# A scheduled attention and mixer kernel: a shorter chain for 64-bit weights, and merged softmax operations

## The chip, the core and the metric

The kernel runs on one core of one Trainium2 chip. The core has a matrix engine (TensorE; its weight loads are a row of their own, PEld, in the profile), a vector engine (VectorE, DVE in the profile), a scalar engine (ScalarE, ACT), GpSimd (POOL) and SyncE (SP), which only issues transfers here. The metric is the device time of one launch in microseconds. Shown are the median of three runs before the change, 1540.35 us, and their ends, 1537.54 and 1543.84 us.

## The reference

Three stages follow one another. All weight matrices and U, V come in 64-bit floats, everything else in 32-bit.

```python
def sm_attn(qq, kk, vv):                       # scale = 1/8
    s = scale * np.matmul(qq, kk.transpose(0, 1, 3, 2))
    a = np.exp(s - np.max(s, axis=-1, keepdims=True))
    a = a / (np.sum(a, axis=-1, keepdims=True) + 1e-09)
    return np.matmul(a, vv)
p_packed = sm_attn(p, k, v)                    # first softmax: 32 packed queries, 576 keys
out = sm_attn(q, p_packed, p_packed)           # second softmax: 576 queries, 32 keys
# out: batch 8, heads 8, 576, 64  ->  x: 8, 576, 512
xk = mu_k * x + (1.0 - mu_k) * x_prev          # x_prev: x shifted by one position
xr = mu_r * x + (1.0 - mu_r) * x_prev
k = np.maximum(xk @ w_k, 0.0)                  # 512 -> 1024
x = 1.0 / (1.0 + np.exp(-(xr @ w_r))) * (k * k @ w_v)
u = x + (x.transpose(0, 2, 1) @ U @ V).transpose(0, 2, 1)     # rank 32 over the positions
return u + np.maximum(u @ w_ch1, 0.0) @ w_ch2  # 512 -> 2048 -> 512
```

## The kernel before

The batches are taken in four pairs. One attention unit is a pair of batches and a pair of heads, so there are 16 units, four to a batch pair. A unit (`attention_steps`) loads k, q and v, transposes them on TensorE, forms the scores of the packed queries in two PSUM banks, takes the first softmax (statistics in the small tile `st`, exponentials in `a1`), multiplies by v to get the packed values `pp`, and then takes the second softmax: 20 groups of 32 keys, 16 of them in one PSUM bank (`psa`) and 4 in another (`psb`), with statistics in `s2` (`s` in the trace) and exponentials in `a2` (`a` in the trace). The output `xo` goes to a scratch array `x_d`. The first four units, those of batch pair 0, run beside one another, staggered; the other twelve run beside the stages that follow.

The second stage works on 12 chunks of 384 rows. It reads `x_d` back (`x`), mixes it (`m`, `xk`, `xr`), and runs matmuls into `psr`, `psk` and `psv`. A chunk needs all four units of its pair, since its contraction is over all heads. The third stage (`psu`, `psh`, `pst`, `psc`) starts at about 739 us of the trace.

A float matrix is used as two parts, `hi` and `lo`, in a rounded 32-bit format, and three products of parts stand for one product. A 64-bit weight reaches that form in the class `Cast`: a transfer brings a tile of 128 rows and 512 64-bit words into a staging buffer `st` (two of them, in rotation, so a third load waits until the first buffer has had its last reader), then a chain of ScalarE and VectorE operations builds the 32-bit value `m` from the high words (`hb`, `top`) and the low words of each number. Twenty tiles (w_r 4, w_k 8, w_v 8) end in a pair of parts (`parts` given); `split` makes these from `m`. Another 32 tiles (w_ch1, w_ch2) and the three pieces of U and V end in `m` itself (`put` given), which for w_ch1 and w_ch2 is stored to scratch and split much later. The name `st` in the trace thus is two things: the 128x512 staging buffer and the narrow statistics tile of the first softmax; and `a` is three (the softmax exponentials and the scratch of the conversion); shapes tell them apart.

No engine order is written out by hand. The program records operations with what they read and write, and `Plan.emit` runs a list scheduler over them with its own table of durations per engine, classes of priority (`cls`), and the banks of PSUM; in this way each engine gets one fixed order of instructions. On SyncE the order is fixed too, so a load that has to wait for its buffer holds up everything that stands behind it. A change of one operation's number or length can thus change the order on all engines.

ScalarE holds one table of functions at a time; `Exp` and `Sigmoid` are in different ones, and an `ACT_TABLE_LOAD` stands between them.

Of the kernel before, what the change touches and what calls it, by code (L numbers as in the profile page):

```python
# [9 lines left out]
F32 = mybir.dt.float32  # L10
F32R = mybir.dt.float32r
I32 = mybir.dt.int32
U32 = mybir.dt.uint32
AF = mybir.ActivationFunctionType
ALU = mybir.AluOpType
# [85 lines left out]
class Plan:  # L101
# [151 lines left out]

    def ts(self, out, a, s1, s2, op0, op1=None, engs=("dve",), cls=None):
        k = {} if op1 is None else {"op1": op1}
        return self.elem(
            engs, lambda e, o, x: e.tensor_scalar(out=o, in0=x, scalar1=s1, scalar2=s2, op0=op0, **k),
            out, [a], self.TC, cls)
# [212 lines left out]
def packed_attention_moe_mixer_kernel(  # L471
# [19 lines left out]
    NP = p.shape[2]  # L491
    P = 128
# [12 lines left out]
    SCALE = 1.0 / float(D) ** 0.5  # L505
# [3 lines left out]
    plan = Plan(nc)  # L509
    add, sub, mul = ALU.add, ALU.subtract, ALU.mult  # L510

    def open_pool(es, name, bufs, side):
        return es.enter_context(tc.tile_pool(name=name, bufs=bufs, side=side, reuse_waits="tile"))
# [19 lines left out]
    def ctile(name, shape, dt=F32):  # L533
        return plan.fixed(const.tile(shape, dt, name=name))

    ident = ctile("ident", [P, P])
    hmask = ctile("hmask", [P, 2, D])
# [8 lines left out]
    def ps_att():  # L546
        return plan.bank(att_banks[0], "psat", att_banks[0] is ps_a)
# [17 lines left out]
    class Bufs:  # L565
        def __init__(self, es, name, side, nbig, first=False):
            self.big_p = Pool(obj=open_pool(es, name + "big", nbig, side), bufs=nbig)
            one = open_pool(es, name + "one", 1, side)
            self.one = Pool(obj=one, bufs=1)
            self.a1 = plan.fixed(one.tile([P, 640], F32, name="a1"))  # L570
            self.pbd = plan.fixed(one.tile([P, 2, D], F32, name="pbd"))
            self.first = first
            self.pools = [self.big_p, self.one]
            for f in (self.a1, self.pbd):
                f.alloc = plan.add((), lambda: None)
                self.one.tiles.append(f)
            self.kin, self.qin, self.vin, self.after = {}, {}, {}, ()
            plan.zero(self.a1[:, 512:640])
            self.kept = None

        def keep(self, plain):
# [53 lines left out]
    def attention_steps(A, u, u_next):  # L635
# [35 lines left out]
        if u_next is not None:  # L671
            A.load_k(u_next, A.after)

        st = plan.tile(A.one, [P, 16], F32, "st", parts=(0, 1))
        yield
        sps = [ps_att() for _ in range(2)]
        for b2 in range(2):
            for h in range(2):
                o = slice(b2 * 64 + h * 32, b2 * 64 + (h + 1) * 32)
# [5 lines left out]
        for b2 in range(2):  # L685
            for h in range(2):
                o = slice(b2 * 64 + h * 32, b2 * 64 + (h + 1) * 32)
                plan.mm(sps[0][o, 256:320], pT[0:64, b2, h * 32:(h + 1) * 32],
                        kt[0:64, h, b2 * 64:(b2 + 1) * 64], start=True, stop=True, skip_group_check=True)
        plan.reduce(st[:, 0:1], sps[0][:, 0:320], ALU.max)  # L690
        plan.reduce(st[:, 1:2], sps[1][:, 0:256], ALU.max)
        plan.tt(st[:, 2:3], st[:, 0:1], st[:, 1:2], ALU.max)
        plan.ts(st[:, 3:4], st[:, 2:3], -SCALE, None, mul)
        a1 = A.a1
        bias = st.at(0)[:, 3:4]
        for r in range(2):
# [3 lines left out]
        for b2 in range(2):  # L700
            r = slice(b2 * 64, (b2 + 1) * 64)
            plan.act(a1[r, 512 + b2 * 64:576 + b2 * 64], sps[0][r, 256:320], AF.Exp,
                     st.at(1)[r, 6:7], bias[r], SCALE)
        plan.reduce(st[:, 7:8], st[:, 4:7], add)
        plan.ts(st[:, 8:9], st[:, 7:8], 1e-9, None, add)
        plan.recip(st[:, 9:10], st[:, 8:9])

        for c in range(3):
            yield
# [25 lines left out]
        for t in range(5):  # L735
            for g in range(4):
                o = t * P + g * 32
# [3 lines left out]
                        start=(t == 0), stop=(t == 4), skip_group_check=True)  # L741
        pp = plan.tile(A.one, [P, P], F32, "pp")
        plan.stt(pp.rearrange("p (h d) -> p h d", h=2), ps[:, 0:D].unsqueeze(1).to_broadcast([P, 2, D]),
                 st[:, 9:10], hmask, mul, mul)
        plan.copy(ppz[:, 0, :], pp)
        if not plain:
            plan.tt(ppz[:, 1, :], pp, ppz[:, 0, :], sub)
# [18 lines left out]
        if A.first:  # L766
            a2 = A.big(F32, "a2", (0, 1))[:, 0:20 * NP].rearrange("p (g k) -> p g k", k=NP)
        else:
            a2 = plan.tile(A.one, [P, 20, NP], F32, "a2", parts=(0, 1))
        s2 = plan.tile(A.one, [P, 4, 20], F32, "s2", parts=(0, 1))  # L770
        for g, src, g0, g1 in ((0, psa, 0, 16), (1, psb[:, 0:P], 16, 20)):
            sv = src.rearrange("p (g k) -> p g k", k=NP)
            av, s = a2.on(g)[:, g0:g1, :], s2.at(g)
            bc = [P, g1 - g0, NP]
            plan.reduce(s[:, 0, g0:g1], sv, ALU.max)
            plan.tt(av, sv, s[:, 0, g0:g1].unsqueeze(2).to_broadcast(bc), sub)
            plan.act(av, av, AF.Exp, scale=SCALE)
            plan.reduce(s[:, 1, g0:g1], av, add)
            plan.ts(s[:, 2, g0:g1], s[:, 1, g0:g1], 1e-9, None, add)
            plan.recip(s[:, 3, g0:g1], s[:, 2, g0:g1])  # L780
            plan.tt(av, av, s[:, 3, g0:g1].unsqueeze(2).to_broadcast(bc), mul)

        a2f = a2.on(0).rearrange("p g k -> p (g k)")
        a2g = a2.on(1).rearrange("p g k -> p (g k)")
        th = A.big(F32 if plain else F32R, "th")
        tl = None if plain else A.big(F32R, "tl")
        yield
# [26 lines left out]
    def attention(A, u, u_next):  # L814
        for _ in attention_steps(A, u, u_next):
            pass


    class Cast:
# [7 lines left out]
        def run(self, srcs, n, put=None, parts=None, after=()):  # L827
            N = self.N
            raw = srcs[0][1].dtype != F32
            st = plan.tile(self.st, [P, N * 2], I32, "st", parts=tuple(range(len(srcs))))  # L830
            for i, (rows, src) in enumerate(srcs):
                s = st.at(i)
                to = s[rows, 0:2 * n] if raw else s[rows, 0:n].bitcast(F32)
                if raw:
                    src = src.bitcast(I32)
                if src.shape[0] > P:
                    to = to.rearrange("p (a c) -> p a c", a=src.shape[0] // P)
                    src = src.rearrange("(a p) c -> p a c", p=P)
                plan.dma(to, src, after=after)
            if not raw:  # L840
                if parts is None:
                    put(st.bitcast(F32))
                else:
                    split(*parts, st.bitcast(F32)[:, 0:n])
                return st.alloc
            r = slice(srcs[0][0].start, srcs[-1][0].stop)
            sv = st.rearrange("p (n t) -> p n t", t=2)[r, 0:n]
            whole = [plan.tile(self.tp, [P, N], F32, tag) for tag in "am"]
            a, m = [t[r, 0:n] for t in whole]
            top = h = sv[:, :, 1].bitcast(F32)  # L850
            plan.act(a, top, AF.Abs)
            plan.stt(h, a, 1.125 * 2.0 ** -15, top, ALU.is_ge, mul)
            plan.act(m, sv[:, :, 0].bitcast(U32), AF.Copy, scale=2.0 ** -52)
            hb, ab = sv[:, :, 1], a.bitcast(I32)
            plan.ts(ab, hb, 3, 0x3FFFFFF8, ALU.logical_shift_left, ALU.bitwise_and)
            plan.stt(ab, hb, -0x40000000, ab, ALU.bitwise_and, ALU.bitwise_or)
            plan.ts(hb, ab, -0x800000, None, ALU.bitwise_and)
            plan.tt(m, m, h, mul)
            plan.tt(m, m, a, add)
            if parts is None:  # L860
                put(whole[1])
            else:
                split(*parts, m)
            return st.alloc

    def split(hi, lo, src, engs=("dve",)):
        plan.copy(hi, src, ("act", "dve"))
        plan.tt(lo, src, hi, sub, engs)
# [42 lines left out]
    plan.cls = 0  # L911
    A0.after = go
    steps = [attention_steps(AX_[u], u, NJ if u == 0 else None) for u in range(NJ)]
    step = 0
    while any(s is not None for s in steps):
# [181 lines left out]
    def tmp_tile():  # L1097
        i = count["tmp"] % 6
        count["tmp"] += 1
        if i < 2:  # L1100
            return plan.tile(m_p, [P, CW], F32, "m", name="tmp")[:, 0:256]
        return plan.tile(tr_p, [P, 256], F32, "tmp")
# [114 lines left out]
    def product(q, f, i, name, fresh):  # L1217

        if fresh:
            bank_abc[name] = plan.bank(ps_c1, "psc1")  # L1220
        ps = bank_abc[name][:, 0:256]
        w, x = load_ws(f, i), ops[q][i]
        n = 0
        for k in range(2):
            for wi, a in PASS:
                plan.mm(ps, half(w, wi)[:, k * P:(k + 1) * P],
                        half(x, a)[:, k * 256:(k + 1) * 256],
                        start=(fresh and n == 0), stop=(n == 5), skip_group_check=True)
                n += 1
        return ps  # L1230
# [114 lines left out]
    for q in range(NQ):  # L1345
# [11 lines left out]
        for f in range(NF):  # L1357
# [4 lines left out]
            a = product(q, f, 0, "a", True)  # L1362
# [3 lines left out]
            s = tmp_tile()  # L1366
# [70 lines left out]
```

## Time and profile before

| What | Value |
|---|---|
| median of three runs | 1540.35 us (1537.54 to 1543.84) |
| span of the profiled execution, first to last instruction | 1538.1 us |
| TensorE busy | 1491.3 us, 97% of the span |
| VectorE busy | 962.4 us, 63% |
| ScalarE busy | 707.1 us, 46% |
| loads of 64-bit tiles on SyncE up to 175 us | 20, the first five of them before 40 us |

The page gives no time of the profiled execution other than its span, which lies 2.25 us under the median of the runs. The shares are means over stages with different limits. The page's line of 40 slices (38.5 us each) shows the stages apart: TensorE has gaps in the first four or five slices and hardly any after. A row of instruction groups gives busy time and the mean of one instruction, and then the idle time of the engine before it. Instructions of one engine overlap at their ends, so that the distance from start to start is a little shorter than the time of one.

### The profile page before, as it was taken

What the parts mean: (1) busy time and instruction counts of PE and PEld (TensorE: products, weight loads), DVE (VectorE), ACT (ScalarE), POOL (GpSimd) and SP (SyncE); (2) the same over time, 40 slices, a digit from 0 to 9 for tenths busy, and PEclk for the clock granted to TensorE, in tenths of its full rate; (3) what the DMA queues carried; (4) which work ended last, traced back from release to release, by engine and by line L of the source; (5) the groups of instructions that cost most, each with busy time, mean ns of one, the idle gap of its engine ahead of it and who ended that gap; (6) DMA issues with size and microseconds to landing.
All of it is one profiled execution on the core that took longest, in us unless ns stands there. A gap on an engine that the chain in (4) does not pass through costs nothing.

```text
span 1538.1 us, 25958 instructions
## 1 busy us (share of the span) xinstructions
PE 1491.3 (97%) x9460; PEld 1303.1 (85%) x9460; DVE 962.4 (63%) x2221; ACT 707.1 (46%) x1635; POOL 270.3 (18%) x522
## 2 busy tenths in 40 slices
PE   6779899999999999999999999999999999999998
PEld 4657688888888888888899999999999899999997
DVE  6888877888778886875745454444535354444533
ACT  5777657656756765665522232323222232322221
POOL 0000000000000000001233333333333333333331
PEclk9779999999999999999999999999999999999999
DMA  9865455555555444656877767686866767676763
GB/s 232 206 156 147 122 141 159 155 165 153 160 149 154 139 152 144 223 206 209 263 178 217 190 172 221 166 239 160 230 165 188 203 166 225 161 219 157 205 170 101
DMA packets 202174, 275.67 MB, mean 179 GB/s; under 512 B 68928, under 2 KB 95872, under 8 KB 202048
## 3 DMA queue, kind: packets, MB, share of 16 engines
q0 software_dynamic: 72576, 132.15, 33.0%
q1 hardware_dynamic: 129472, 141.87, 31.1%
q8 instruction: 76, 1.25, 0.3%
q14 instruction: 50, 0.41, 0.1%
HBM read 221.45 MB, written 52.50 MB: 178 GB/s over the span
## 4 chain that ended last, share of the span: by engine, by line
PE 91%; DMA 3%; DVE 2%; SPq 2%; ACT 2%; issue 1%; DVEq 0%
PE psc L197 49%; PE psk L197 13%; PE psv L197 13%; PE psr L197 6%; PE psat L197 4%; PE psat L209 2%; SPq L312 2%; PE psu L197 1%; PE psh L197 1%; PE pst L209 1%; DMA vin<-in_v_dram 1%; DMA s<-w_d 1%; DMA st<-in_moe_w_k_dram 0%; ACT a L230 0%; DMA kin<-in_k_dram 0%
## 5 line engine op out<-in xcount | busy, mean ns | idle before, releaser
L197 PE MATMUL psc<-w,hid 128*128 128x512 f32 x1728 | 446.2, 393 | 1.3 <-ACT xu L281 1.3
L197 PEld LDWEIGHTS psc<-ob,wb 128*128 128x128 f32 x3024 | 406.9, 190 | 26.7
L197 PE MATMUL psc<-ob,wb 128*128 128x256 f32 x3024 | 420.8, 283 | 0.0
L312 POOL DMA_DIRECT2D wb<-ws_d x504 | 267.2, 531 | 593.6 <-PE psc L197 498.6
L197 PEld LDWEIGHTS psc<-w,hid 128*128 128x128 f32 x1728 | 306.2, 189 | 52.0 <-ACT xu L281 1.6
L197 PE MATMUL psk<-xk,wk 128*128 128x384 f32 x1152 | 232.3, 344 | 3.4 <-ACT sq L230 2.4
L197 PE MATMUL psv<-wv,kk 128*128 128x512 f32 x864 | 231.7, 402 | 3.7 <-DVE wv L251 2.2
L197 PEld LDWEIGHTS psk<-xk,wk 128*128 128x128 f32 x1152 | 202.4, 189 | 13.9 <-ACT sq L230 3.3
L251 DVE TENSOR_TENSOR tmp<-tmp,psc 128x256 f32<-128x256 f32 x288 | 120.5, 419 | 143.4 <-PE psc L197 142.2
L230 ACT ACTIVATE hid<-tmp 128x256 fp32r<-128x256 f32 x216 | 85.2, 417 | 262.9 <-DVE tmp L251 262.7
L197 PEld LDWEIGHTS psv<-wv,kk 128*128 128x128 f32 x864 | 157.4, 189 | 37.9 <-DVE wv L251 4.2
L266 DVE SCALAR_TENSOR_TENSOR hid<-psc,hid 128x256 fp32r<-128x256 f32 x72 | 30.5, 424 | 188.3 <-ACT hid L230 188.3
L197 PE MATMUL psr<-wr,xr 128*128 128x512 f32 x432 | 114.7, 408 | 6.9 <-ACT r L281 2.7
L281 ACT ACTIVATE tmp<-psc 128x256 f32<-128x256 f32 x144 | 54.6, 379 | 126.5 <-PE psc L197 126.5
L197 PEld LDWEIGHTS psr<-wr,xr 128*128 128x128 f32 x432 | 80.7, 193 | 26.5 <-ACT r L281 3.8
L266 DVE SCALAR_TENSOR_TENSOR hid<-tmp,hid 128x256 fp32r<-128x256 f32 x216 | 86.3, 422 | 23.6 <-ACT hid L230 19.1
L304 POOL MEMSET x<- 128x8 f32 x4 | 0.5, 134 | 563.6 <-DVE m L263 385.9
L251 DVE TENSOR_TENSOR kk<-sq,kk 128x384 fp32r<-128x384 f32 x96 | 52.6, 552 | 41.3 <-ACT kk L281 41.1
L230 ACT ACTIVATE sq<-psk 128x384 f32<-128x384 f32 x96 | 46.4, 487 | 67.8 <-PE psk L197 66.9
L230 ACT ACTIVATE hid<-psc 128x256 fp32r<-128x256 f32 x72 | 27.5, 382 | 102.6 <-PE psc L197 102.6
L263 DVE SCALAR_TENSOR_TENSOR m<-x,mu_t,m 128x384 f32<-128x384 f32 x96 | 57.8, 611 | 6.6 <-ACT m L230 6.4
L230 ACT ACTIVATE m<-x,om_t 128x384 f32<-128x384 f32 x96 | 57.3, 610 | 7.5 <-DVE xk L251 3.8
(152 smaller groups left out, 1670.4 us busy)
## 6 DMA issues: line engine op xcount, KB each, us to landing
wb<-ws_d POOLq DMA_DIRECT2D x504, 256.0 KB, 3.1
st<-in_moe_w_ch_dram SPq DMA_DIRECT2D x32, 512.0 KB, 4.3
ws_d<-wb SPq DMA_DIRECT2D x56, 256.0 KB, 3.2
qin<-in_q_dram SPq DMA_DIRECT2D x32, 288.0 KB, 5.7
x_d<-xo SPq DMA_DIRECT2D x16, 576.0 KB, 3.1
x_d<-x SPq DMA_DIRECT2D x36, 256.0 KB, 3.4
u<-x_d SPq DMA_DIRECT2D x36, 256.0 KB, 5.8
out_dram<-u SPq DMA_DIRECT2D x36, 256.0 KB, 3.6
```

What stands on the lines that cost most here:

```text
L197: self.nc.tensor.matmul(o, l, r, start=start, stop=stop, **k)
L209: self.nc.tensor.transpose(out.get(), in_.get(), ident.get())
L230: self.nc.scalar.activation(o, in_.get(), func, **k)
L251: return self.elem(engs, lambda e, o, x, y: e.tensor_tensor(out=o, in0=x, in1=y, op=op), out, [a, b], self.TT, cls)
L263: ("dve",), lambda e, o, x, y, z: e.scalar_tensor_tensor(out=o, in0=x, scalar=z, in1=y, op0=op0, op1=op1), out, [a, b, s], {"dve": (1.042, ...
L266: ("dve",), lambda e, o, x, y: e.scalar_tensor_tensor(out=o, in0=x, scalar=s, in1=y, op0=op0, op1=op1), out, [a, b], self.TT, cls)
L281: self.nc.scalar.activation(o, i, AF.Copy)
L304: (self.nc.gpsimd if eng == "pool" else self.nc.vector).memset(o, 0.0)
L312: (self.nc.sync if eng == "sp" else self.nc.gpsimd).dma_start(out=o, in_=i)
```

## The change

The conversion: the comparison that set small numbers to zero becomes a maximum against the same constant, and the multiplication by the high word's float value moves into the last step. For a weight with parts, `hi` is no longer rounded from the finished value but built from the high word with its low bits masked off, and `lo` from the 9 bits left over plus the low word. ScalarE no longer converts the low words. In that form both the masked word and the low words stay in the staging buffer until the chain's last operation, which reads `top`.

The first softmax: `st` is a fixed tile; two small operations become one with a second scalar operand, and the constant 1e-9 stands in a fourth column of the sums. The second softmax: maximum and subtraction stay in two groups (16 and 4), everything after them is one operation over all 20.

```diff
@@ Plan.ts @@
+        if isinstance(s1, Ref):
+            return self.elem(
+                engs, lambda e, o, x, y: e.tensor_scalar(out=o, in0=x, scalar1=y, scalar2=s2, op0=op0, **k),
+                out, [a, s1], self.TC, cls)
...
@@ Bufs.__init__ @@
+            self.st = plan.fixed(one.tile([P, 16], F32, name="st"), (0, 1))
...
+            plan.ts(self.st.at(1)[:, 7:8], self.a1[:, 512:513], 1e-9, None, add)
...
@@ attention_steps, Cast.run @@
-        st = plan.tile(A.one, [P, 16], F32, "st", parts=(0, 1))
+        st = A.st
...
-        plan.reduce(st[:, 0:1], sps[0][:, 0:320], ALU.max)
-        plan.reduce(st[:, 1:2], sps[1][:, 0:256], ALU.max)
-        plan.tt(st[:, 2:3], st[:, 0:1], st[:, 1:2], ALU.max)
-        plan.ts(st[:, 3:4], st[:, 2:3], -SCALE, None, mul)
+        s0, s1 = st.at(0), st.at(1)
+        plan.reduce(s0[:, 0:1], sps[0][:, 0:320], ALU.max)
+        plan.reduce(s0[:, 1:2], sps[1][:, 0:256], ALU.max)
+        plan.ts(s0[:, 3:4], s0[:, 0:1], s0[:, 1:2], -SCALE, ALU.max, mul)
...
-        plan.reduce(st[:, 7:8], st[:, 4:7], add)
-        plan.ts(st[:, 8:9], st[:, 7:8], 1e-9, None, add)
-        plan.recip(st[:, 9:10], st[:, 8:9])
+        plan.reduce(s0[:, 8:9], s1[:, 4:8], add)
+        plan.recip(s0[:, 9:10], s0[:, 8:9])
 
...
-                 st[:, 9:10], hmask, mul, mul)
+                 s0[:, 9:10], hmask, mul, mul)
...
-            av, s = a2.on(g)[:, g0:g1, :], s2.at(g)
-            bc = [P, g1 - g0, NP]
-            plan.reduce(s[:, 0, g0:g1], sv, ALU.max)
-            plan.tt(av, sv, s[:, 0, g0:g1].unsqueeze(2).to_broadcast(bc), sub)
-            plan.act(av, av, AF.Exp, scale=SCALE)
-            plan.reduce(s[:, 1, g0:g1], av, add)
-            plan.ts(s[:, 2, g0:g1], s[:, 1, g0:g1], 1e-9, None, add)
-            plan.recip(s[:, 3, g0:g1], s[:, 2, g0:g1])
-            plan.tt(av, av, s[:, 3, g0:g1].unsqueeze(2).to_broadcast(bc), mul)
-
-        a2f = a2.on(0).rearrange("p g k -> p (g k)")
-        a2g = a2.on(1).rearrange("p g k -> p (g k)")
+            plan.reduce(s2.at(g)[:, 0, g0:g1], sv, ALU.max)
+            plan.tt(a2.on(g)[:, g0:g1, :], sv,
+                    s2.at(g)[:, 0, g0:g1].unsqueeze(2).to_broadcast([P, g1 - g0, NP]), sub)
+        plan.act(a2, a2, AF.Exp, scale=SCALE)
+        plan.reduce(s2[:, 1, :], a2, add)
+        plan.ts(s2[:, 2, :], s2[:, 1, :], 1e-9, None, add)
+        plan.recip(s2[:, 3, :], s2[:, 2, :])
+        plan.tt(a2, a2, s2[:, 3, :].unsqueeze(2).to_broadcast([P, 20, NP]), mul)
+
+        a2f = a2g = a2.rearrange("p g k -> p (g k)")
...
-            top = h = sv[:, :, 1].bitcast(F32)
+            top, hb, low = sv[:, :, 1].bitcast(F32), sv[:, :, 1], sv[:, :, 0]
+            ab, mb = a.bitcast(I32), m.bitcast(I32)
             plan.act(a, top, AF.Abs)
-            plan.stt(h, a, 1.125 * 2.0 ** -15, top, ALU.is_ge, mul)
-            plan.act(m, sv[:, :, 0].bitcast(U32), AF.Copy, scale=2.0 ** -52)
-            hb, ab = sv[:, :, 1], a.bitcast(I32)
-            plan.ts(ab, hb, 3, 0x3FFFFFF8, ALU.logical_shift_left, ALU.bitwise_and)
-            plan.stt(ab, hb, -0x40000000, ab, ALU.bitwise_and, ALU.bitwise_or)
-            plan.ts(hb, ab, -0x800000, None, ALU.bitwise_and)
-            plan.tt(m, m, h, mul)
-            plan.tt(m, m, a, add)
+            plan.ts(a, a, 1.125 * 2.0 ** -15, None, ALU.max)
             if parts is None:
+                plan.ts(mb, ab, 3, 0x3FFFFFF8, ALU.logical_shift_left, ALU.bitwise_and)
+                plan.stt(ab, hb, -0x40000000, mb, ALU.bitwise_and, ALU.bitwise_or)
+                plan.ts(hb, ab, -0x800000, None, ALU.bitwise_and)
+                plan.stt(m, low.bitcast(U32), 2.0 ** -52, top, mul, mul)
+                plan.tt(m, m, a, add)
                 put(whole[1])
             else:
-                split(*parts, m)
+                hi, lo = parts
+                plan.ts(mb, ab, 3, 0x3FFFF000, ALU.logical_shift_left, ALU.bitwise_and)
+                plan.stt(mb, hb, -0x40000000, mb, ALU.bitwise_and, ALU.bitwise_or)
+                plan.copy(hi, m)
+                plan.ts(hb, mb, -0x800000, None, ALU.bitwise_and)
+                plan.ts(ab, ab, 0x1FF, None, ALU.bitwise_and)
+                plan.stt(a, ab, 2.0 ** 32, low.bitcast(U32), mul, add)
+                plan.stt(lo, a, 2.0 ** -52, top, mul, mul)
```

How the scheduler's order moves is shown at three places. Names in them: `wr`, `wk_0`, `wk_1`, `wv` are the weight parts, `s_221` and `a_916` (after: `a_876`) the statistics and exponentials of the fourth unit's second softmax, `x_d_65` the scratch of batch pair 0. A line number of the kernel after is 4 higher in the same helper.

VectorE, where the fourth unit's second softmax ends, before:

```order
L270 TENSOR_REDUCE s_221<-a_916 128x16
L270 TENSOR_REDUCE s_221<-a_916 128x4
L257 TENSOR_SCALAR s_221<-s_221 128x16
L251 TENSOR_TENSOR wk_0_184<-m,wk_0_184 128x512
L257 TENSOR_SCALAR s_221<-s_221 128x4
L274 RECIPROCAL s_221<-s_221 128x16
L274 RECIPROCAL s_221<-s_221 128x4
L257 TENSOR_SCALAR om_t<-mu_t 128x8
L251 TENSOR_TENSOR a_916<-a_916,s_221 128x512
L251 TENSOR_TENSOR a_916<-a_916,s_221 128x128
```

And after:

```order
L274 TENSOR_REDUCE s_221<-a_876 128x20
L270 SCALAR_TENSOR_TENSOR wk_0_187<-a,st 128x512
L251 TENSOR_TENSOR xr<-m,xr 128x384
L261 TENSOR_SCALAR s_221<-s_221 128x20
L261 TENSOR_SCALAR a<-a 128x512
L278 RECIPROCAL s_221<-s_221 128x20
L261 TENSOR_SCALAR m<-a 128x512
L251 TENSOR_TENSOR a_876<-a_876,s_221 128x640
```

Eight statistics rows became four. The conversion beside them is one tile further back than before (the third of the four w_k tiles, `wk_0_187`, where it was the fourth, `wk_0_184`), while the first `xr` of the next stage now stands ahead of this softmax's end.

SyncE, from the load of the second w_k tile on, before:

```order
L312 DMA st<-in_moe_w_k_dram 128x1024
L312 DMA x_d_65<-xo 128x1152
L312 DMA st<-in_moe_w_k_dram 128x1024
L312 DMA x<-x_d_65 128x384
L312 DMA x<-x_d_65 128x2x63
L312 DMA st<-in_moe_w_k_dram 128x1024
L312 DMA kin<-in_k_dram 128x2x256 x2
```

And after, from the same place:

```order
L316 DMA x_d_65<-xo 128x1152
L316 DMA st<-in_moe_w_k_dram 128x1024
L316 DMA x<-x_d_65 128x384
L316 DMA x<-x_d_65 128x2x63
L316 DMA st<-in_moe_w_k_dram 128x1024
L316 DMA x_d_65<-xo 128x1152
L316 DMA x<-x_d_65 128x384
L316 DMA x<-x_d_65 128x2x63
L316 DMA st<-in_moe_w_k_dram 128x1024
L316 DMA kin<-in_k_dram 128x2x256 x2
```

The first unit's store moved ahead of the second w_k load, and the second unit's store and read-back ahead of the fourth.

ScalarE, around the first chunk's three sigmoids (`r<-r`), before:

```order
L230 ACT_TABLE_LOAD
L230 ACTIVATE r<-r 128x512 x3
L281 ACTIVATE xk<-m 128x384
L230 ACT_TABLE_LOAD
L230 ACTIVATE a_729<-a_729 128x512
L230 ACTIVATE a_729<-a_729 128x128
```

And after:

```order
L230 ACTIVATE a_635<-a_635 128x640
L285 ACTIVATE xk<-m 128x384
L285 ACTIVATE wk_1_1105<-m 128x512
L285 ACTIVATE r<-psr 128x512
L230 ACT_TABLE_LOAD
L230 ACTIVATE r<-r 128x512 x3
L230 ACTIVATE m<-x,om_t 128x384
```

The fifth unit's exponential (`a_729`, after: `a_635`) stood behind the sigmoids with a second table load of its own; it now stands ahead of them, and that second load comes later, before another unit's first softmax.

## Rows read from the trace of the kernel before

**Rows 1.** The page: the span, then 40 equal slices of it, in tenths

```profile
span 1538.1 us, 25958 instructions
...
PE   6779899999999999999999999999999999999998
...
PEclk9779999999999999999999999999999999999999
```

**Rows 2.** Stretches: length, busy PE, PEld, DVE, ACT, POOL, granted clock, DMA share, GB/s

```profile
0.00:44.00 44.00, 28.93 (x306) 22.98 (x307) 28.66 (x80) 25.87 (x71) 1.32 (x11) 0.92 1.01 227
44.00:80.00 36.00, 26.96 (x211) 20.77 (x211) 31.52 (x85) 25.10 (x68) 0.00 (x0) 0.67 0.72 205
80.00:120.00 40.00, 31.54 (x168) 25.07 (x167) 32.43 (x76) 28.62 (x63) 0.00 (x0) 0.78 0.55 137
120.00:175.00 55.00, 48.71 (x318) 36.70 (x317) 48.95 (x110) 37.34 (x88) 0.00 (x0) 1.00 0.54 158
...
44.00:175.00 131.00, 107.21 (x693) 82.54 (x692) 112.90 (x270) 91.06 (x218) 0.00 (x0) 0.84 0.59 164
175.00:1538.00 1363.00, 1355.15 (x8465) 1197.54 (x8463) 820.88 (x1873) 590.15 (x1348) 269.00 (x511) 1.00 0.64 179
```

**Rows 3.** Chain that ended last, 44 to 175 us: start, length, what

```profile
208 pieces in order of time: start us, us, what
43.85 0.26 ACT at L281
...
88.07 7.64 DMA st<-in_moe_w_k_dram
...
105.02 1.28 ACT L230
...
108.41 1.28 ACT L230
...
173.24 1.86 PE psr L197 x7
```

**Rows 4.** Groups by form, 0 to 175 us: the conversion (busy us, mean ns)

```profile
L251 DVE TENSOR_TENSOR m<-m,st 128x512 f32<-128x512 f32 x20 | 13.7, 683 | 0.0
...
L257 DVE TENSOR_SCALAR a<-st 128x512 int32<-128x512 int32 x20 | 8.2, 415 | 0.0
...
L230 ACT ACTIVATE m<-st 128x512 f32<-128x512 uint32 x20 | 13.5, 673 | 0.7 <-DVE wv L251 0.6
```

**Rows 5.** The same view: the softmaxes

```profile
L270 DVE TENSOR_REDUCE s<-a 128x16 f32<-128x512 f32 x6 | 4.1, 680 | 2.6 <-ACT a L230 2.6
...
L251 DVE TENSOR_TENSOR a<-a,s 128x512 f32<-128x512 f32 x6 | 4.0, 672 | 0.0
...
L270 DVE TENSOR_REDUCE s<-a 128x4 f32<-128x128 f32 x6 | 1.7, 277 | 0.0
...
L251 DVE TENSOR_TENSOR st<-st 128x1 f32<-128x1 f32 x7 | 1.1, 151 | 0.0
...
L274 DVE RECIPROCAL s<-s 128x4 f32<-128x4 f32 x6 | 1.0, 163 | 0.0
...
L230 ACT ACTIVATE a<-a 128x512 f32<-128x512 f32 x6 | 3.8, 627 | 3.1 <-DVE a L251 3.1
...
L230 ACT ACTIVATE a<-a 128x128 f32<-128x128 f32 x6 | 1.8, 304 | 0.0
```

**Rows 6.** Timeline of VectorE at 44 us: start, length, what

```profile
44.74 0.15 DVE L257 TENSOR_SCALAR st<-st 128x1 f32<-128x1 f32 x1
44.80 0.15 DVE L251 TENSOR_TENSOR st<-st 128x1 f32<-128x1 f32 x1
44.87 0.68 DVE L251 TENSOR_TENSOR a<-psat,s 128x512 f32<-128x512 f32 x1
```

**Rows 7.** Waits of SyncE's queue, 0 to 175 us: total, times, longest

```profile
SPq L312 <- DVE m L251: 44.4, 11, 13.1
```

More of the change, by code (lines that the diff above doesn't have):

```diff
@@ L571, in __init__ @@
             self.pbd = plan.fixed(one.tile([P, 2, D], F32, name="pbd"))
+            self.st = plan.fixed(one.tile([P, 16], F32, name="st"), (0, 1))
             self.first = first
             self.pools = [self.big_p, self.one]
-            for f in (self.a1, self.pbd):
+            for f in (self.a1, self.pbd, self.st):
                 f.alloc = plan.add((), lambda: None)
```

## The prediction

> **What bounds the kernel now.** I read the line of 40 slices first, then the stretches around its weak end, then the chain of waits inside that end, and only then single groups. The slices show TensorE below nine tenths in the first three of 40 and once more at 154 us, and nowhere else; its granted clock is lowest in slices two and three, at seven tenths [rows 1]. The stretches say the same in us: from 175 us to the end TensorE is busy for 1355.15 of 1363 us at a clock of 1.00, while VectorE has work for 820.88 and ScalarE for 590.15 [rows 2]. Nothing that this change saves on VectorE or ScalarE after 175 us can shorten that: 7.85 us of TensorE idle are there in all. So the 32 weight tiles of w_ch1 and w_ch2 and the last ten attention units, all converted or computed after 175 us, count for nothing, and TensorE covers them. Should that cover go, the stretch after 175 us would show it as idle time beyond 7.85 us.
>
> Before 175 us the picture is another. From 0 to 44 us the transfers are full (DMA share 1.01, 227 GB/s): what arrives sets the pace there, VectorE is busy for 28.66 of 44 us, and I give the change nothing in it. From 44 to 175 us, 131 us, TensorE is busy for 107.21, at a mean clock of 0.84; VectorE for 112.90 (86%), ScalarE for 91.06 [rows 2]. Here no engine is the bound throughout. The chain of waits for the same stretch [rows 3] has 208 pieces; summed by engine over all of them, TensorE holds 55.1 us, transfers 22.3, ScalarE 21.6, VectorE 21.2, SyncE's queue 6.4, and gaps without a visible cause 4.4. That is where the time can come from: 42.8 us of VectorE and ScalarE on the path, and behind them a VectorE that is 86% full. Two pieces of ScalarE are of a kind of their own, 1.28 us each at 105.02 and 108.41: table loads around the first sigmoids.
>
> **The conversion.** Twenty tiles have parts, and all twenty are done before 175 us (each row of rows 4 has x20). Old chain on VectorE, per tile: four two-input operations before the split and the subtraction in it, five at the 683 ns of the row shown, and two one-input operations at 415 ns: 5 x 683 + 2 x 415 = 4245 ns [rows 4]. New chain: three two-input ones (the sign merge, the sum of the small bits, the last product) and four one-input ones (maximum, shift, two masks): 3 x 683 + 4 x 415 = 3709 ns. Saved: 536 ns a tile. The one new kind is the sum that takes one integer operand times a constant plus another unsigned one. The trace shows no such form; its nearest rows are the two-input ones at 683 and, below, the one-input ones at 415, and above, two of the two-input ones after each other, 1366. I take 683; the ends would move the saving to 0.80 us or to -0.15 us a tile. ScalarE drops the conversion of the low words, 673 ns a tile [rows 4]; its rounding copy of `hi` stays, only earlier in the chain.
>
> Of the twenty tiles five are loaded before 40 us, so 15 lie in the stretch: VectorE 15 x 0.536 = 8.0 us, ScalarE 15 x 0.673 = 10.1 us.
>
> The number of VectorE operations in this chain is seven before and seven after; rows of 683 ns against 415 ns for the same 512 columns show that the kind of operation, not the count, sets its time [rows 4]. The Trainium skill ("VectorE: DVE Perf Modes", Rules for kernel authors) says of chained VectorE operations not to fuse for speed and to minimise their count; by that alone the conversion would gain nothing. The trace disagrees for tiles of 512 columns.
>
> **The softmaxes.** Six second softmaxes run before 175 us, five of them after 44 us. The sum over 640 columns instead of 512 and 128: slope (680 - 277) / 384 = 1.05 ns a column, so 814 ns for 957, less 0.14; the last product likewise, 0.14 (672 for its large row; its small one taken as the sum's 277); the reciprocal of 4 columns (163) goes, less about 0.03 for a wider other one; one small addition, near 0.15, goes [rows 5]. About 0.57 us by durations. But short rows start 0.06 and 0.07 us after one another [rows 6], since they overlap their neighbours, so four rows fewer cost VectorE about 4 x 0.08 less than that sum says: 0.25 us at the low end. First softmax: two rows of about 0.15 go, 0.3 us by duration, 0.13 by start to start. Together 0.4 to 0.9 us a unit; I take 0.6 and five units: 3.0 us of VectorE. ScalarE's exponential: 627 + 304 becomes 627 + 128 x 0.84 = 735 (slope (627 - 304) / 384), 0.2 us a unit, 1.0 us in all.
>
> The merge adds one wait: the exponential of the 16 groups now waits for the other bank's maximum and subtraction too, and in the queue of ScalarE whatever stands behind it waits along. Nearest rows: nothing, since the small ones were executed in the shadow of the large exponential, or the small exponential and sum, 0.1 + 0.13 us, longer; at the far end two small VectorE rows of 0.28 on top, 0.8 us a unit. I take 0.1 us and five units, 0.5 us lost. The four new additions of 1e-9 at the start stand before the first transfer has landed, at no cost; without that cover each is one row of 0.15 us.
>
> **The table load.** The order on ScalarE moves the fifth unit's exponential ahead of the first sigmoids. One of the two loads on the path, 1.28 us [rows 3], moves to a later place; there TensorE has matmuls of the first chunk queued. I count 1.3 us, with 0 as the other end.
>
> **The sum.** VectorE loses 8.0 + 3.0 = 11.0 of 112.9 us in the stretch, 9.7%; ScalarE 11.1 of 91.06, 12%. Lower end: only the pieces on the chain shrink by these shares: 21.2 x 9.7% + 21.6 x 12% = 2.1 + 2.6 = 4.7 us. Upper end: VectorE is what everything in the stretch waits for, and all of its 11.0 us return. The stretch's 86% of VectorE is nearer to a full engine than to an idle one, yet TensorE holds 55.1 us of the chain and transfers 22.3, so I stay in the lower half: 6.2 us, plus 1.3 for the table load, less 0.5 for the added wait: 7.0 us. The span of the profiled execution, 1538.1 us, would become 1531.1 us; the median of the runs is 2.25 us above that span, so 1533.3 us, rounded 1533 us.
>
> **Rivals.**
>
> The clock comes back as well. In 44 to 80 and 80 to 120 us TensorE was busy for 26.96 and 31.54 us at a granted clock of 0.67 and 0.78 [rows 2], a mean between its two levels of 1.2 and 2.4 GHz, after gaps of its own; at full clock that work would take 26.96 x 0.33 + 31.54 x 0.22 = 15.8 us less. With all 11.0 us of VectorE and a third of these, 5, plus the table load, 17 us: 1523 us. For it: these stretches are those where VectorE is fullest (31.52 of 36 us). Against it: transfers set some of the gaps (7.64 us for one w_k load at 88.07 [rows 3]), and they stay. The Trainium skill ("TensorE: Matmul & The Clock Gate", Part 1: The HAM clock gate) says that the throttled clock is the default and that activity releases it; the trace agrees in so far as the clock is 1.00 in all of the busy stretch behind 120 us, and by that rule this case would follow from fewer gaps.
>
> The gain is hidden. If transfers, TensorE's own work and the new order's different waits set the stretch, no more than 0 to 3 us come out: 1537 to 1540 us. For it: TensorE's 55.1 and the transfers' and SyncE's 28.7 us are two thirds of the chain. The Trainium skill's rule on the count of operations, named above, would lead here. Against it: the two other engines' 42.8 us.
>
> The staging buffer is held longer, and the kernel gets slower. Before, its last reader was the multiplication by the high word: 3 x 683 + 2 x 415 = 2.88 us of VectorE work after the absolute value. Now it is the last operation of the whole chain, 3.71 us: 0.83 us more a tile, in which nothing may be loaded into it. SyncE already waited 44.4 us, 11 times, for just that multiplication [rows 7], and what is queued behind such a wait on SyncE are the stores and read-backs of `x_d`, on which the first chunk depends. Eighteen loads wait for a buffer's earlier tile, in two buffers; nine holds in a row at 0.83 are 7.5 us, with the gain eaten by the same waits: 1548 us. It decides if SyncE's waits for that last product grow by more than about 7 us over the 44.4. Against it: VectorE has less to do in all, so each step is reached sooner; and the new order lets the first units' stores pass the w_k loads.
>
> **How the numbers follow.** The forecast has 0.45, with a range of its own of 1529 to 1537; the clock's case 0.22; the hidden gain 0.20; the held buffer 0.13. About 0.5%, 7.7 us, is what a measurement can tell from no change: faster means under 1532.7 us. The clock's case and nearly half of the forecast lie there: 0.22 + 0.21 = 0.43. The rest of the forecast and the hidden gain are within 0.5%: 0.44. The held buffer is slower: 0.13. The range of 8 in 10 reaches from 1522 us, with most of the clock's case in it, to 1546 us, which leaves out the full price of the held buffer and little else; the unknown form's ends, 15 x 0.26 = 4 us up and 15 x 0.69 = 10 us down, and the planner's new order on all engines lie in it.
>
> **What would show it.** In the profile after: the x20 group of the integer sum near 683 ns, and no 673 ns group of the low words on ScalarE; VectorE's busy sum up to the last `wv` part less by about 11 us; TensorE's idle time and low clock before 175 us less by about 7 us, and still about 8 us idle after it; one table load gone from the path at the first sigmoids. Wrong would be: TensorE idle in the long stretch after 175 us, a new sum of the order of 1 us, or SyncE waiting longer for the weight parts than it did for the product.

## The result, and the profile after

The changed kernel took 1526.46 us (median of four runs, 1525.6 to 1530.27), the kernel before 1539.78 us beside it: a ratio of 0.9899, 95% interval 0.9876 to 0.9923, so 1.0% faster. The forecast was 1533 us with a range of 1522 to 1546: the direction and the range hold, the gain is about twice the 7.0 us of the sum (13.3 us by the medians, 15.6 us by the ratio).

The page of the kernel after, span and slices:

```profile
span 1523.8 us, 25783 instructions
...
PE   6789999999999999999999999999999999999998
...
PEclk9879999999999999999999999999999999999999
```

The span is 14.3 us shorter than that of [rows 1]. TensorE reaches nine tenths by the fourth slice and stays there; before, it fell back in the fifth.

The stretches of the kernel after, columns as in [rows 2]:

```profile
0.00:44.00 44.00, 28.28 (x321) 21.56 (x321) 29.31 (x79) 25.77 (x72) 1.31 (x11) 1.00 0.99 224
44.00:80.00 36.00, 26.64 (x232) 18.90 (x236) 31.55 (x78) 23.04 (x67) 0.00 (x0) 0.82 0.79 227
80.00:120.00 40.00, 33.92 (x208) 28.08 (x201) 34.24 (x75) 29.63 (x61) 0.00 (x0) 0.82 0.58 163
...
160.00:1523.80 1363.80, 1357.16 (x8468) 1199.01 (x8467) 810.66 (x1823) 573.71 (x1298) 268.25 (x511) 1.00 0.65 179
```

The long full stretch is the same length as before (1363.8 us here from 160 us, 1363 there from 175 us), with 6.64 us of TensorE idle in it where there were 7.85. The whole gain lies ahead of it. In 44 to 80 us the granted clock is 0.82 for 0.67, in 80 to 120 us it is 0.82 for 0.78, and in 0 to 44 us, where the prediction gave the change nothing, it is 1.00 for 0.92. VectorE is as full as before from 44 to 80 and from 80 to 120 us (31.55 and 34.24 us, for 31.52 and 32.43): its savings did not show as idle time. The last weight part (`wv`) was ready at 160.74 us, where before it was ready at 168.11 us. Up to there, first the kernel before and then the one after:

```profile
0.00:168.11 168.11, 129.42 (x948) 100.65 (x949) 134.87 (x332) 113.08 (x279) 1.32 (x11) 0.86 0.70 179
```

```profile
0.00:160.74 160.74, 125.65 (x997) 96.81 (x997) 130.41 (x314) 104.50 (x265) 1.31 (x11) 0.92 0.75 196
```

VectorE's busy sum up to that point fell by 4.5 us, where the prediction's sign said about 11. What else VectorE had done by then differs between the two orders, so this sum does not measure the saving by itself.

The chain that ended last, 44 to 160 us, as in [rows 3]:

```profile
192 pieces in order of time: start us, us, what
42.52 4.72 DMA x_d<-xo
...
76.06 6.92 DMA x<-x_d
...
97.95 1.28 ACT L230
...
119.28 1.28 ACT L230
```

Summed over all its pieces TensorE holds 44.9 us (55.1 in the 131 us of before), ScalarE 20.3 (21.6), VectorE 17.9 (21.2), transfers 26.6 (22.3), SyncE's queue 3.9 (6.4). Two stores and two read-backs of `x_d`, 20.7 us, are on the path now, where before it was one store of 4.20 us; this fits the order on SyncE, in which they moved ahead of `w_k` loads. Both table loads are still on it, the second only 11 us later than before.

The changed groups, 0 to 160 us, as in [rows 4, 5] (`tensor_tensor` and `activation` stay at L251 and L230 in the kernel after; the operation with two scalars has a line of its own, L258):

```profile
L270 DVE SCALAR_TENSOR_TENSOR m<-st,m 128x512 int32<-128x512 int32 x20 | 13.7, 687 | 0.1
L270 DVE SCALAR_TENSOR_TENSOR a<-a,st 128x512 f32<-128x512 int32 x20 | 13.7, 686 | 0.0
...
L261 DVE TENSOR_SCALAR a<-a 128x512 f32<-128x512 f32 x20 | 8.5, 423 | 7.5 <-ACT a L230 7.5
...
L251 DVE TENSOR_TENSOR a<-a,s 128x640 f32<-128x640 f32 x6 | 4.9, 819 | 0.0
L274 DVE TENSOR_REDUCE s<-a 128x20 f32<-128x640 f32 x6 | 4.9, 816 | 0.4 <-ACT a L230 0.4
...
L258 DVE TENSOR_SCALAR st<-st 128x1 f32<-128x1 f32 x7 | 1.4, 198 | 0.1
```

The integer sum, the one form that the trace before did not show, took 686 ns (683 taken). The sum over 640 columns took 816 (814 worked out). The small operation with two scalars took 198 ns; it stands for two of about 150.

SyncE's waits for VectorE ahead of loads into the staging buffer, 0 to 175 us:

```profile
SPq L316 <- DVE s L278: 11.6, 1, 11.6
SPq L316 <- DVE s L261: 11.0, 1, 11.0
SPq L316 <- DVE wk L270: 10.6, 3, 7.0
...
SPq L316 <- DVE wv L270: 4.6, 4, 2.7
...
SPq L316 <- DVE m L261: 2.9, 2, 2.1
SPq L316 <- DVE st L274: 2.8, 1, 2.8
SPq L316 <- DVE st L278: 2.1, 1, 2.1
```

Only two of these rows name the buffer's new last readers, the weight parts `wk` and `wv`. The others name an operation that VectorE had begun behind such a reader. The timeline of VectorE and of SyncE at the longest wait shows this:

```profile
99.88 0.68 DVE L270 SCALAR_TENSOR_TENSOR wk<-a,st 128x512 fp32r<-128x512 f32 x1
100.48 0.27 DVE L278 RECIPROCAL s<-s 128x20 f32<-128x20 f32 x1
```

```profile
100.59 0.34 SPq L316 DMA_DIRECT2D st<-in_moe_w_k_dram  x1
```

The load was issued 0.03 us after the end of `wk` at 100.56 us, while the reciprocal still ran. The second wait, 11.0 us, ended likewise: `wv` was ready at 141.68 us and the load was issued at 141.71 us. Together the rows make 45.6 us.

The kernel before has such a row too, behind the product that [rows 7] counts. The first piece of U was loaded into the buffer at 164.18 us, 0.03 us after the end of a product at 164.15 us, and the wait stands under the operation that follows:

```profile
SPq L312 <- DVE st L257: 8.9, 1, 8.9
```

```profile
163.47 0.68 DVE L251 TENSOR_TENSOR m<-m,st 128x512 f32<-128x512 f32 x1
164.07 0.42 DVE L257 TENSOR_SCALAR st<-a 128x512 int32<-128x512 int32 x1
```

So SyncE waited for the buffer's last reader for 44.4 + 8.9 = 53.3 us before and for 45.6 us after.

### The profile page after: what moved, and what is told of

Same layout as the page of the kernel before. It is cut to its first block, busy times and chain, and to the rows that moved or that the text cites. A ratio compares the mean times of both kernels' runs of the same rounds, so it can differ in the third digit from the quotient of the medians.

```text
span 1523.8 us, 25783 instructions
## 1 busy us (share of the span) xinstructions
PE 1482.1 (97%) x9460; PEld 1295.4 (85%) x9460; DVE 940.3 (62%) x2133; ACT 677.6 (44%) x1560; POOL 269.6 (18%) x522
## 4 chain that ended last, share of the span: by engine, by line
PE 91%; DMA 3%; DVE 2%; ACT 2%; SPq 1%; issue 1%; DVEq 0%; ACTq 0%
PE psc L197 49%; PE psk L197 13%; PE psv L197 13%; PE psr L197 6%; PE psat L197 4%; PE psat L209 2%; PE psh L197 1%; PE psu L197 1%; PE pst L209 1%; SPq L316 1%; DMA x_d<-xo 1%; DMA st<-in_moe_w_r_dram 1%; DMA x<-x_d 1%; DMA s<-w_d 1%; ACT a L230 1%
## 5 line engine op out<-in xcount | busy, mean ns | idle before, releaser
L251 DVE TENSOR_TENSOR tmp<-tmp,psc 128x256 f32<-128x256 f32 x288 | 120.8, 420 | 143.2 <-PE psc L197 141.9
L230 ACT ACTIVATE hid<-tmp 128x256 fp32r<-128x256 f32 x216 | 85.2, 417 | 262.9 <-DVE tmp L251 262.9
L251 DVE TENSOR_TENSOR kk<-sq,kk 128x384 fp32r<-128x384 f32 x96 | 52.9, 553 | 42.0 <-ACT kk L285 41.4
L230 ACT ACTIVATE sq<-psk 128x384 f32<-128x384 f32 x96 | 46.3, 486 | 62.2 <-PE psk L197 59.5
L230 ACT ACTIVATE hid<-psc 128x256 fp32r<-128x256 f32 x72 | 27.5, 381 | 101.2 <-PE psc L197 101.2
L230 ACT ACTIVATE m<-x,om_t 128x384 f32<-128x384 f32 x96 | 57.2, 609 | 14.9 <-DMA x<-x_d 6.8
```

Of the source, the lines that this page charges most:

```text
L230: self.nc.scalar.activation(o, in_.get(), func, **k)
L251: return self.elem(engs, lambda e, o, x, y: e.tensor_tensor(out=o, in0=x, in1=y, op=op), out, [a, b], self.TT, cls)
```

## The experiments

The theory: conversion and softmaxes relieve VectorE and ScalarE before 175 us, and the conversion carries most of it. Rivals: the softmaxes do; one of the two engines alone does; the held buffer takes part back; or the gain is the luck of one order of the planner, since every edit reorders all engines. All ratios are to the kernel before on the same chip. Its median beside these runs was 1542.57 to 1543.29 us, some 3 us above that of the first comparison, which the expectations in us did not know; so the ratios decide.

**The conversion alone** (all of the diff in `Cast.run`, nothing else).

> The new conversion alone, both softmaxes as before. Theory (the conversion's relief of VectorE and ScalarE before 175 us pays for most): of the 14 us between the kernels at least 9 come, 1526 to 1531 us. Rival (the merged softmaxes pay): no more than 4 us come, 1536 to 1540 us. Rival (it is the planner's new order, by chance): any time between 1522 and 1545 us, with no sum of parts.

1539.98 us, ratio 0.9984 (0.9971 to 0.9997): 2.5 us of 15.6. The theory's figure fails, and the time is the one that the softmax rival expected.

**The softmaxes alone** (all of the diff but `Cast.run`).

> The merged softmaxes alone, the conversion as before. Theory: VectorE loses about 3 us before 175 us and the time falls by 1 to 5 us, 1535 to 1539 us. Rival (the softmaxes pay): by 8 us or more, under 1532 us. Rival (chance of the order): anything from 1522 to 1545 us, so that the gains of this run and of the conversion alone do not add up to 14 within 4 us.

1545.99 us, 1.0022 (1.0007 to 1.0038): slower, so the softmax rival fails too. The parts add up to -0.16% + 0.22%, the whole is -1.0%. This is what the rival of the order's luck expected.

**ScalarE's part alone**, on the kernel before:

```diff
-            plan.act(m, sv[:, :, 0].bitcast(U32), AF.Copy, scale=2.0 ** -52)
...
-            plan.tt(m, m, h, mul)
+            plan.stt(m, sv[:, :, 0].bitcast(U32), 2.0 ** -52, h, mul, mul)
```

> The kernel before, with one edit: ScalarE no longer converts the low words; the multiplication on VectorE takes them as they are and holds the factor as its constant. VectorE's count and lengths stay, ScalarE loses 673 ns a tile. Theory (both engines' pieces on the chain count): about half of the conversion's gain, 3 to 6 us, 1534 to 1537 us. Rival (VectorE alone is what is waited for): within 2 us of the kernel before, 1538 to 1542 us.

1536.51 us, 0.9975 (0.9962 to 0.9989): 3.9 us, as the theory had it, and more than the whole conversion gave. Taken alone it means little, as the orders below show.

**VectorE's saving given back**, on the changed kernel:

```diff
                 plan.stt(lo, a, 2.0 ** -52, top, mul, mul)
+                plan.stt(m, a, 1.0, a, mul, mul)
```

> The changed kernel, with one idle two-input operation of 512 columns more on VectorE after each of the 20 tiles with parts (683 ns, written to scratch that nothing reads), which gives back the 536 ns saved there and 147 ns more; ScalarE's saving and the chain's length to the weight parts stay. Theory (VectorE's load before 175 us counts): 7 to 13 us of the gain are lost, 1533 to 1540 us. Rival (it was the shorter chain and ScalarE, not the load): no more than 3 us lost, 1526 to 1530 us.

1535.89 us, 0.9954 (0.994 to 0.9968): 0.55% above the changed kernel, so 8.5 us of the gain are lost, inside the theory's 7 to 13; but the second order of the changed kernel and its early release below, with no work added, also lose 0.5%. Inconclusive.

**The kernel before in another order.** Same instructions, one number of the planner (its delay from VectorE to VectorE):

```diff
-           "dve": {"pe": 202.0, "act": 128.0, "pool": 155.0, "dve": 127.0},
+           "dve": {"pe": 202.0, "act": 128.0, "pool": 155.0, "dve": 100.0},
```

> The kernel before with the same instructions in another order: only the planner's own number for the delay from VectorE to VectorE is 100 instead of 127 ns. It measures how far a new order alone moves the time. Theory: the order alone moves it by less than 5 us, 1535 to 1545 us. Rival (the gain is the luck of an order): by 8 us or more in either direction.

1549.18 us, 1.0045 (1.0028 to 1.0063), 7 us slower: more than the theory's 5, under the rival's 8.

**The changed kernel with the same edit.**

> The changed kernel with the same edit of the planner's number. Theory: within 5 us of the changed kernel, 1521 to 1531 us, and still 8 us or more under the reordered kernel before. Rival (the luck of an order): 1533 us or more.

1534.67 us, 0.9947 (0.9931 to 0.9962): 0.48% or 7.4 us above the changed kernel, where the theory allowed 5, so by its time alone this run is on the rival's side (1533 us or more). Against the reordered kernel before it is 0.9947 / 1.0045 = 0.990, or 14.5 us faster, where the theory wanted 8 or more. Single times move with the order by half a per cent; the difference between the kernels stays at 1.0% in this order.

**The buffer released earlier**, on the changed kernel:

```diff
-                plan.ts(hb, mb, -0x800000, None, ALU.bitwise_and)
                 plan.ts(ab, ab, 0x1FF, None, ALU.bitwise_and)
                 plan.stt(a, ab, 2.0 ** 32, low.bitcast(U32), mul, add)
-                plan.stt(lo, a, 2.0 ** -52, top, mul, mul)
+                plan.ts(mb, mb, -0x800000, None, ALU.bitwise_and)
+                plan.stt(lo, a, 2.0 ** -52, m, mul, mul)
```

> The changed kernel, with the masked high word written to scratch instead of back into the staging buffer, and after the sum of the low words; the buffer's last reader is then that sum, about 1.1 us of VectorE work earlier (two operations), at the same count and kinds of operations. Theory (loads are waited for no more than before, the held buffer costs little): within 3 us of the changed kernel, 1523 to 1530 us. Rival (the held buffer takes back part of the gain): 4 to 8 us faster, 1518 to 1522 us.

1535.68 us, 0.9949 (0.9931 to 0.9968): 0.5% slower than the changed kernel, where neither side had it. SyncE's waits for the new last reader, `a`:

```profile
SPq L316 <- DVE a L270: 36.9, 6, 11.6
```

That is some 8 us less than the 45.6 us of the changed kernel, so SyncE did wait less for the buffer. Still the kernel was no faster: what the release is worth is hidden in the order's own effect, or the waits are covered.

**Each transposition of the first four units twice**, on the changed kernel (`tr` in place of `plan.transpose` in `attention_steps`):

```diff
+        def tr(*a):
+            for _ in range(2 if u < NJ else 1):
+                plan.transpose(*a)
```

> The changed kernel, with each TensorE transposition of the first four units issued twice (the second writes the same values to the same place): some 120 instructions more, a good 7 us of TensorE work at full clock, all before 90 us. Theory (TensorE waits there, and its clock is lower where it waits): the granted clock between 44 and 120 us rises over 0.82 and the time stays within 3 us of the changed kernel, 1523 to 1530 us, or falls below. Rival (TensorE's own work in the first units is on the path): 5 us or more slower, 1531 us and up.

1536.79 us, 0.9971 (0.9954 to 0.9989): 0.7% slower than the changed kernel. Its stretches, columns as before:

```profile
44.00:80.00 36.00, 26.77 (x273) 20.66 (x272) 30.53 (x75) 22.95 (x62) 0.00 (x0) 0.98 0.73 207
80.00:120.00 40.00, 36.20 (x207) 28.58 (x207) 33.58 (x76) 31.41 (x68) 0.00 (x0) 0.89 0.47 137
```

With more TensorE work put in (273 matmuls for 232 in the first row), the granted clock rises from 0.82 to 0.98 and from 0.82 to 0.89. Over 44 to 120 us it is 0.93, above the 0.71 to 0.82 of both kernels in all three of their orders. So this stretch's clock does follow what TensorE does in it, as the theory expected. But the time rose too; the rival's side of the expectation, that this work is on the path, is the one met, by 0.7% where an order alone moves half a per cent.

**The conversion alone in the second order** (100 ns).

> The new conversion alone, in the order that the planner makes with 100 ns in place of 127. With the reordered kernel before at 1.0045 and the reordered changed kernel at 0.9947 of the kernel before, it completes a second order for the four combinations. Theory (the conversion carries the effect, and the small gain of the conversion alone in the first order was that order's bad luck): 0.993 to 0.999 of the kernel before, half or more of the way from 1.0045 to 0.9947. Rival (the two parts only pay together): 1.001 to 1.006.

1538.54 us, 0.9975 (0.9957 to 0.9993): as the theory had it, 0.7% under 1.0045.

**The softmaxes alone in the second order.**

> The merged softmaxes alone, in the order that the planner makes with 100 ns in place of 127. Theory (the softmaxes are a small part): within 0.3% of the reordered kernel before, 1.0015 to 1.0075 of the kernel before. Rival (the softmaxes pay, or the parts pay only together and this order chose otherwise): under 1.000.

1536.3 us, 0.9963 (0.9942 to 0.9985): 0.8% under 1.0045, against the theory and as the rival had it. In the first order they cost 0.2%.

**Both kernels in a third order** (150 ns).

> The kernel before in a third order: the planner's number for the delay from VectorE to VectorE is 150 instead of 127 ns, nothing else. Theory: within 0.5% of the kernel before, 0.995 to 1.005, and 0.6% or more above the changed kernel with the same edit. Rival (the effect is the luck of an order): no more than 0.3% above the changed kernel with the same edit, or below it.

> The changed kernel in a third order, with the same edit, 150 instead of 127 ns. Theory: 0.988 to 0.996 of the kernel before. Rival (the luck of an order): 0.998 or more.

1548.75 us, 1.0041 (1.0027 to 1.0054), and 1530.25 us, 0.9911 (0.9881 to 0.9941): as the theory had it, 0.9911 / 1.0041 = 0.987.

Both kernels and their parts in all orders (named by the planner's number in ns), as ratios to the kernel before:

| | order 127 | order 100 | order 150 |
|---|---|---|---|
| neither part | 1 | 1.0045 | 1.0041 |
| conversion | 0.9984 | 0.9975 | not run |
| softmaxes | 1.0022 | 0.9963 | not run |
| both | 0.9899 | 0.9947 | 0.9911 |

What follows: the whole change is worth 1.0% in two orders and 1.3% in the third, and the slowest order of the changed kernel (0.9947) is faster than the fastest of the kernel before (1); that it is only an order's luck falls. How the gain divides between the parts is not settled: conversion alone 0.16% and 0.70%, softmaxes alone -0.22% and 0.82%, with an order's own scatter of about half a per cent on every single figure. Over the two orders the means are 0.43% for the conversion, 0.30% for the softmaxes and 1.0% for both. Which engine's relief pays is not shown either. No kernel tried was faster than the changed one.

Where the time sits can be read from one row, 0 to 200 us, for each order. The kernel before in its three orders (127, 100, 150):

```profile
0.00:200.00 200.00, 160.26 (x1166) 126.86 (x1167) 161.09 (x401) 135.71 (x329) 1.32 (x11) 0.88 0.66 169
```

```profile
0.00:200.00 200.00, 156.62 (x1118) 123.99 (x1119) 155.65 (x380) 132.88 (x323) 1.32 (x11) 0.85 0.64 166
```

```profile
0.00:200.00 200.00, 161.38 (x1139) 127.70 (x1140) 159.81 (x392) 130.94 (x320) 1.31 (x11) 0.83 0.65 166
```

And the changed kernel, in the same orders:

```profile
0.00:200.00 200.00, 164.91 (x1305) 130.36 (x1306) 160.89 (x388) 132.06 (x326) 1.31 (x11) 0.93 0.69 182
```

```profile
0.00:200.00 200.00, 166.45 (x1233) 132.16 (x1234) 154.69 (x375) 127.62 (x315) 1.32 (x11) 0.87 0.67 178
```

```profile
0.00:200.00 200.00, 171.45 (x1264) 133.67 (x1265) 160.22 (x391) 130.79 (x322) 1.31 (x11) 0.91 0.68 181
```

Each row is one execution. TensorE's idle time is 200 less its busy time: 39.7, 43.4 and 38.6 us before, 35.1, 33.6 and 28.6 after, a mean of 40.6 against 32.4. What the clock costs is estimated as the busy time by what is missing to 1.00 (the row's clock is a mean over idle time too): 19.2, 23.5 and 27.4 us before, 11.5, 21.6 and 15.4 after, 23.4 against 16.2. So of 15.4 us in these 200, 8.2 are waits and 7.2 the clock; the mean spans differ by 17.2 us (1544.8 and 1527.6). Idle time is lower in all three orders after than in any before; the clock's part scatters more.

The clock's part does not rest on these six executions alone. The mean granted clock of the whole span, over the executions that the ratios use and whose clock is on record, was 0.983 for the kernel before and 0.987 for the changed one (four executions), 0.976 and 0.984 in the second order, 0.978 and 0.986 in the third. Within one kernel it moved about as much from execution to execution (0.978 to 0.988 in 23 of the kernel before), so a single profile cannot tell such differences.

The same row for VectorE's saving given back, and for ScalarE's part alone, is no help in dividing the gain:

```profile
0.00:200.00 200.00, 160.62 (x1209) 126.60 (x1209) 161.21 (x380) 127.56 (x314) 1.32 (x11) 0.89 0.65 173
```

```profile
0.00:200.00 200.00, 167.49 (x1188) 131.23 (x1188) 162.58 (x405) 126.05 (x311) 1.31 (x11) 0.90 0.65 171
```

TensorE was idle for 39.4 us in the first, as in the kernel before, and for 32.5 us in the second, as in the changed one. Both spare ScalarE the low words and neither spares VectorE the conversion (the first has the merged softmaxes besides); with much the same work on both engines they fall on opposite sides.

## Why the prediction was right, and where its size was off

That nothing after 175 us matters, and that all of the gain comes ahead of it, held: the long stretch kept its length and its few us of idle time.

The price of the form not seen before held to within 3 ns. VectorE's saving a tile: by the new rows 3 x 686 + 4 x 420, 3738 ns, for 4245, so 0.51 us where 0.54 was counted.

The table load, counted at 1.3 us, brought nothing: it moved by 11 us and stayed on the chain. The added wait of the merged softmax, counted at 0.5 us, cannot be read off: TensorE waited 4.3 us, 3.0 at the longest, for the last products of second softmaxes before 200 us, for 2.6 and 1.8 in the kernel before; but the kernel before waited 6.3 and 3.7 us for them in its other two orders, the changed kernel 3.9 us in its second and not visibly in its third.

The step that was mis-sized is the sum: "Lower end: only the pieces on the chain shrink by these shares", and the choice of the lower half, with the clock in a rival. The forecast put 6.2 us on waits and nothing on the clock. Over three orders waits fell by 8.2 us and the clock's cost by 7.2. The clock's case, at 1523 us, had priced nearly that (5 us of clock, 17 in all) and was nearer to the outcome than the forecast; it had 0.22. Between the two kernels as they are the clock's part is 19.2 - 11.5 = 7.7 us by the 200 us rows and the waits' 4.6. Of the 7.7 us, 2.3 lie in 0 to 44 us (28.93 us at 0.92 before, 1.00 after), which the prediction left out; that may be the order's luck, since in the second order the clock of this stretch fell, from 0.84 to 0.77. The Trainium skill ("TensorE: Matmul & The Clock Gate", Part 1: The HAM clock gate) has activity release a throttled clock; here the trace agrees in so far as the granted clock of 44 to 80 us was 0.82 in the changed kernel and 0.98 in the run with more TensorE work.

The held buffer falls as a reason to be slower: its sign, waits longer by 7 us, did not come. SyncE's waits for the buffer's last reader went from 53.3 to 45.6 us, of which the prediction's row of 44.4 us had left out one of 8.9. What the later release still costs stays open, since the earlier one came with another order. The hidden gain falls with 1.0 to 1.3% in three orders.

What the prediction did not see is the size of the order's own effect. It named the new order as something that lies in the range; the runs give it half a per cent, as much as the forecast's whole gain. That the gain is the change's and not an order's rests on the three pairs, not on the first comparison. That it comes by the relief of VectorE and ScalarE, in the shares that the sum gave them, is argued and not shown: the parts did not separate. The range held in part because it was 24 us wide.

## What to carry to other kernels

Where a scheduler orders the instructions, an edit's own worth has to be measured over several orders of both kernels, the same perturbation on each side: single orders here differ by up to 0.5%, pairs agree on 1.0 to 1.3%. The gain came here only in the stretch where TensorE waits, and there in two parts, as fewer waits (8.2 us) and as a higher granted clock (7.2 us), so both belong into the sum. A row of waits names what the profile takes for the releaser; before a sum of such rows is believed, the timeline around the longest of them shows whether the name is right.

## What the runs showed that was not expected

- A small VectorE operation with one scalar from a tile beside its constant took 198 ns on one column, where the small ones with a constant alone took about 146: the merge of two small operations saved 0.1 us and not 0.15.
- TensorE's granted clock in one and the same stretch, 0 to 200 us, ranged from 0.83 to 0.93 over one execution of each of two kernels in three orders, whose work differs by little; by the estimate above that is 16 us of time between the ends (27.4 and 11.5).
